# One chunk per turn from the start, and the gates and scans of block 7 moved up, in a recurrence-plus-maxout kernel

## Chip, cores, metric

The kernel runs on one core of a Trainium2 chip (trn2). The metric is the device time of one execution in microseconds (us). Kernels that are compared ran on the same chip in alternating rounds. A difference of 1 us is 0.26% here, so single executions mean little.

## The reference

```
sig = 1 / (1 + exp(-f_logit));  f = lb + (1 - lb) * sig;  i = 1 - f       # x, f_logit: (4, 6144, 256) fp32
for t in range(S):  h = f[:, t] * h + i[:, t] * x[:, t];  y[:, t] = h      # a recurrence per channel
h1 = y @ w1;  h2 = y @ w2                                                  # (24576, 256) @ (256, 1024)
out = maximum(h1, h2) @ w_out                                              # (1024, 256), fp32 out
```

## The kernel before

The 24576 tokens are 48 blocks of 512. Blocks 0 to 3 are chunks 0 to 3, loaded straight into SBUF. From block 4 on, two blocks are a *pair* and come as one chunk of 1024 tokens: pair 2 (blocks 4, 5) is chunk 4, pair 3 (blocks 6, 7) is chunk 5, and so on to chunk 25. A chunk takes these steps:

1. **Cast** (`fetch`): a DMA issued by POOL (GpSimd) reads fp32 and writes fp16 to one of two scratch areas in HBM, once for `f_logit` and once for `x`.
2. **Transpose** (`cross`): a DMA issued by SP (SyncE) turns each half into SBUF, with channels on the partitions (`fT`, `xT`). POOL waits for `fT`, then issues the next chunk's cast. That closes a loop: cast, transpose, next cast.
3. **Gate** on ACT (ScalarE): a sigmoid in four pieces, two for each block. Piece q covers time half q // 2 of the chunk and channel half q % 2.
4. On DVE (VectorE): **decay** and **drive** (small elementwise), then two **scans** for each block. `scan10` and `scan11` are the two channel halves of the pair's second block.
5. **First layer** on TensorE, 512 columns for each matmul, with a relu on ACT.
6. **Second layer**. From pair 2 on, the two blocks of a pair share seven products instead of eight. Their inputs are four **sums** of relu results, made on DVE (`sum3`, `sum1`, `sum2`, `sum4`, 1.4 us each). The sevenths of pair p run while the first layer of pair p + 1 runs.

TensorE instructions of a stage stand in 16 *slots*. `seq` holds (key, DVE work); slot n emits the work whose key is below 9(n + 1). Every engine takes its instructions in the order in which this loop emits them.

```
    def cross(*cs):
        if len(cs) > 1:                       # only cross(4, 5)
            nc.sync.dma_start(out=seen[:], in_=scratch[1][cs[-1] % NSCR][CH - 1 : CH, 0:16])
        for c in cs:
            for s in range(2):
                dst = inpool.tile([P, KC, CH], HALF, name=("fT", "xT")[s])
                nc.sync.dma_start_transpose(out=dst[:], in_=scratch[s][c % NSCR][:])
                held[c, s] = dst
        pool_waits(held[cs[-1], 0][:, 0, 0:1])
        if cs[-1] + 1 < NCHUNK:
            for s in range(2):
                fetch(cs[-1] + 1, s)
    # ... (cut)
        for p in range(PAIR0, NPAIR):         # PAIR0 = 2
            first = p == PAIR0
            more = p + 1 < NPAIR
            seq = [(27, scans[p]["scan10"]), (36, scans[p]["scan11"]), (112, lambda: sum3(p))]
            if more:
                scans[p + 1] = pair_scans(p + 1)
                seq += [(64, scans[p + 1]["decay0"]), (66, scans[p + 1]["drive0"]),
                        (70, scans[p + 1]["scan00"]), (84, scans[p + 1]["scan01"]),
                        (131, scans[p + 1]["decay1"]), (133, scans[p + 1]["drive1"])]
            if not first:
                seq += [(9, lambda: sum1(p - 1)), (18, lambda: sum2(p - 1)), (50, lambda: sum4(p - 1))]
                queue += sevenths(p - 1)
            seq.sort(key=lambda e: e[0])
            gates = {4: 0, 6: 1, 12: 2, 14: 3} if more else {}
            for slot in range(2 * FC):
                first_layer(2 * p + slot // FC, slot % FC)
                # ... (cut: evictions of block 3, the steps of the sevenths)
                if slot == 2 and p + 3 < NPAIR:
                    cross(blocks[2 * p + 6][3])
                if slot in gates:
                    pair_gate(p + 1, gates[slot])
                while seq and seq[0][0] < (slot + 1) * 9:
                    seq.pop(0)[1]()
```

Of the kernel before, what the change touches and what calls it, by code (L numbers as in the profile page):

```python
# [10 lines left out]
HALF = mybir.dt.float16  # L11
# [3 lines left out]
P = 128  # L15
# [3 lines left out]
def kernel(  # L19
# [10 lines left out]
    nc = tc.nc  # L30
# [4 lines left out]
    KC = D // P  # L35
    FC = DFF // P
    TB = 512
    CH = 1024
# [5 lines left out]
    blocks = []  # L44
    for b in range(B):
# [3 lines left out]
        for nt in sizes:  # L49
            first = len(blocks)  # L50
# [5 lines left out]
    NCHUNK = len(chunks)  # L56
# [4 lines left out]
    PAIR0 = 2  # L61
    NPAIR = NBLK // 2
    KH = FC // 2

    const = ctx.enter_context(tc.tile_pool(name="const", bufs=1))
# [4 lines left out]
    inpool = ctx.enter_context(tc.tile_pool(name="inp", bufs=4))  # L70
# [12 lines left out]
    NSCR = 2  # L83
# [8 lines left out]
    held = {}  # L92
# [3 lines left out]
    def fetch(c, s):  # L96
        b, t0, nt, _ = chunks[c]
        src = srcs[s][b, t0 : t0 + nt, :]
        if by_xbar(c, s):
            nc.gpsimd.dma_start(  # L100
                out=pieces(scratch[s][c % NSCR][:]), in_=pieces(src)
            )
        else:
            nat = inpool.tile([P, TB // P, D], HALF, name=("fT", "xT")[s])
            nc.gpsimd.dma_start(
                out=nat[:].rearrange("p i d -> p (i d)"),
                in_=src.rearrange("(p i) d -> p (i d)", p=P),
            )
            held[c, s] = nat
# [31 lines left out]
                    )  # L141
            raws[k, s] = dst[:].rearrange("p k i m -> p k m i")

    def cross(*cs):


        if len(cs) > 1:
            nc.sync.dma_start(
                out=seen[:], in_=scratch[1][cs[-1] % NSCR][CH - 1 : CH, 0:16]
            )  # L150
        for c in cs:
            for s in range(2):
                dst = inpool.tile([P, KC, CH], HALF, name=("fT", "xT")[s])
                nc.sync.dma_start_transpose(out=dst[:], in_=scratch[s][c % NSCR][:])
                held[c, s] = dst
        pool_waits(held[cs[-1], 0][:, 0, 0:1])
        if cs[-1] + 1 < NCHUNK:
            for s in range(2):
                fetch(cs[-1] + 1, s)

    def turn_steps(j):
        b, t0, nb, c, o = blocks[j]
# [156 lines left out]
    om = const.tile([P, KC], FP32)  # L319
    nom = const.tile([P, KC], FP32)  # L320
    lbc = const.tile([P, KC], FP32)
    seen = const.tile([1, 16], HALF)
    waited = const.tile([P, 1], FP32)
    warm = const.tile([P, 1], FP32)
    wob = wpool.tile([P, FC, D], HALF)
# [21 lines left out]
    def pool_waits(t):  # L347
        nc.gpsimd.tensor_copy(out=waited[:], in_=t)  # L348
# [315 lines left out]
    with tc.manual_schedule():  # L664
        nc.scalar.dma_start(out=lbc[:], in_=lower_bound.rearrange("(h p) -> p h", p=P))
        nc.vector.tensor_copy(out=ident[:], in_=ident_f[:])
        nc.scalar.activation(out=warm[:], in_=ident_f[:, 0:1], func=AF.Sigmoid)
        fetch_first(0)
        fetch_first(1)
        for g in range(NG):  # L670
            fetch_w(g)
        pool_waits(w1n[0][:, 0, 0:1])
        nc.gpsimd.dma_start(
            out=wob[:].rearrange("p (g q) c -> p g (q c)", g=NG),
            in_=moe_w_out.rearrange("(g p q) c -> p g (q c)", g=NG, q=NQ),
        )
        for c in range(1, 6):
            for s in range(2):
                fetch(c, s)
        wt = ps_d.tile([P, 2, 2 * TB], HALF, name="dT")  # L680
        for q in range(8):
            nc.tensor.transpose(wt[:, 0, 0:P], ident[:], ident[:])
        first_bf16(0, 0, nc.vector.tensor_copy)
        first_bf16(0, 1, nc.vector.tensor_copy)
        nc.vector.tensor_scalar_add(out=nom[:], in0=lbc[:], scalar1=-1.0)
        nc.vector.tensor_scalar(
            out=om[:], in0=lbc[:], scalar1=-1.0, scalar2=1.0, op0=ALU.mult, op1=ALU.add
        )
        first_turn(0)
        first_recurrence(0)  # L690
        first_bf16(1, 0, nc.scalar.copy)
        first_bf16(1, 1, nc.scalar.copy)
        first_turn(1)
        first_recurrence(1)
        for q in range(24):
            nc.tensor.transpose(wt[:, 0, 0:P], ident[:], ident[:])
        scale_w1(0)
        half_w1(0, nc.scalar.copy)
        scale_w1(1)
        pt0 = turn_w1(0)  # L700
        for pair in range(2):
            make_wd(0, pair)
            for fc in range(2 * pair, 2 * pair + 2):
                first_layer(0, fc)
        half_w1(1, nc.vector.tensor_copy)
        pt1 = turn_w1(1)
        for pair in range(2):
            make_wd(1, pair)
            for fc in range(4 + 2 * pair, 6 + 2 * pair):
                first_layer(0, fc)  # L710
        keep_w1T(0, pt0)
        keep_w1T(1, pt1)
        steps = turn_steps(1)
        make_w13(0)
        turn(steps[:8])
        gate(1)
        make_w13(1)
        turn(steps[8:])
        for step in scan_steps(1):
            step()  # L720
        cross(4, 5)
        for fc in range(FC):
            if fc == 4:
                turn(turn_steps(2))
                gate(2)
            if fc == 6:
                first_layer(1, 0)
                first_layer(1, 1)
            if fc < 7:
                second_layer(0, fc)  # L730
        for step in scan_steps(2):
            step()
        for step in make_sevens():
            step()
        for fc in range(2, FC):
            first_layer(1, fc)
            if fc == 3:
                second_layer(0, 7)
        turn(turn_steps(3))
        gate(3)  # L740
        early = scan_steps(3)
        for fc in range(FC):
            first_layer(2, fc)
            second_layer(1, fc)
            if fc < 4:
                early[fc]()
        cross(6)
        scans = {PAIR0: pair_scans(PAIR0)}
        gates = {0: 0, 1: 1, 4: 2, 5: 3}
        order = {  # L750
            2: ("decay0", "drive0"),
            3: ("scan00",),
            4: ("scan01",),
            6: ("decay1",),
            7: ("drive1",),
        }
        for fc in range(FC):
            first_layer(3, fc)
            second_layer(2, fc)
            if fc in gates:  # L760
                pair_gate(PAIR0, gates[fc])
            for t in order.get(fc, ()):
                scans[PAIR0][t]()

        queue, due = [], 0
        pieces3, piece = (1, 3, 5, 9, 11, 13, 15), 0
        for p in range(PAIR0, NPAIR):
            first = p == PAIR0
            more = p + 1 < NPAIR
            seq = [  # L770
                (27, scans[p]["scan10"]),
                (36, scans[p]["scan11"]),
                (112, lambda: sum3(p)),
            ]
            if more:
                scans[p + 1] = pair_scans(p + 1)
                seq += [
                    (64, scans[p + 1]["decay0"]),
                    (66, scans[p + 1]["drive0"]),
                    (70, scans[p + 1]["scan00"]),  # L780
                    (84, scans[p + 1]["scan01"]),
                    (131, scans[p + 1]["decay1"]),
                    (133, scans[p + 1]["drive1"]),
                ]
            if not first:
                seq += [
                    (9, lambda: sum1(p - 1)),
                    (18, lambda: sum2(p - 1)),
                    (50, lambda: sum4(p - 1)),
                ]  # L790
                queue += sevenths(p - 1)
            seq.sort(key=lambda e: e[0])
            gates = {4: 0, 6: 1, 12: 2, 14: 3} if more else {}
            for slot in range(2 * FC):
                first_layer(2 * p + slot // FC, slot % FC)
                if first and slot in pieces3 or p == PAIR0 + 1 and slot == 1:
                    second_layer(2 * PAIR0 - 1, piece)
                    piece += 1
                if p > PAIR0 + 1 or (p == PAIR0 + 1 and slot >= LAG):
                    due += NSEV / (2 * FC)  # L800
                    while due >= 1:
                        due -= 1
                        queue.pop(0)()
                if slot == 2 and p + 3 < NPAIR:
                    cross(blocks[2 * p + 6][3])
                if slot in gates:
                    pair_gate(p + 1, gates[slot])
                while seq and seq[0][0] < (slot + 1) * 9:
                    seq.pop(0)[1]()
        for step in queue:  # L810
            step()
        p = NPAIR - 1
        sum1(p)
        sum2(p)
        sum4(p)
        for step in sevenths(p):
            step()
# [30 lines left out]
```

## Time and profile before

| | before |
|---|---|
| time, median of 4 runs beside the changed kernel | 379.67 us (379.19 to 379.68) |
| span of the profiled execution | 377.7 us |
| all 4136 matmuls at their back-to-back spacing (estimate) | 363.1 us |
| TensorE starts later than that spacing, sum | 8.0 us |
| of that, between 20 and 360 us | 0.4 us |

From the profile's page (span; busy time and share; the chain that ended last, by engine):

```profile
span 377.7 us, 9593 instructions
PE 367.9 (97%) x4136; PEld 279.8 (74%) x4136; DVE 338.7 (90%) x410; ACT 302.4 (80%) x410; POOL 35.6 (9%) x79
...
PE 94%; DVE 3%; DMA 1%; issue 0%; SPq 0%; ACT 0%; DVEq 0%
```

TensorE is the limit, and busy time alone cannot tell how tight it is, so I used starts. In the timeline a run of matmuls that waits for nothing starts one every 0.216 us at 512 columns and every 0.056 us at 128. A *late start* below is the spacing of two starts minus that value. The one late start in the middle of the run is here.

61.99 - 61.37 - 0.216 = 0.40 us late: the first layer of block 7 waits for `scan11`. DVE, over the stretch before it (start, length, line, operation; in brackets its idle time and what ended it), has hardly a gap:

```profile
53.18 1.47 DVE L506 TENSOR_TENSOR S<-r 128x2560 f16<-128x2560 f16 x1
54.56 0.61 DVE L213 TENSOR_SCALAR ff<-u,nom 128x512 f16<-128x512 f16 x2
55.09 0.69 DVE L223 TENSOR_TENSOR v<-u,xT 128x1024 f16<-128x1024 f16 x1
56.08 0.69 DVE L496 COPY osb<-ps 128x512 f32<-128x512 f32 x1 [0.30 <-PE ps L487]
56.68 1.48 DVE L506 TENSOR_TENSOR S<-r 128x2560 f16<-128x2560 f16 x1
58.08 1.48 DVE L506 TENSOR_TENSOR S<-r,S 128x2560 f16<-128x2560 f16 x1
59.48 2.45 DVE L230 TENSOR_TENSOR_SCAN r<-ff,r,v 128x512 f16<-128x512 f16 x2
```

In order: `sum3`, decay, drive, the last eviction of block 3, `sum1` (56.68), `sum2` (58.08), `scan10` and `scan11` (59.48). `scan11` ends at 61.93, 0.35 us after it is wanted at 61.58.

The chain that ended last runs through just this piece (start, us, what):

```profile
56.08 0.69 DVE osb L496
56.77 2.80 DVE S L506 x2
59.57 2.38 DVE r L230 x2
61.95 0.04 issue
61.99 0.38 PE dT L441
```

SP's queue, first part (issue time, length of the issue): the tiny read `seen`, four transposes, then stores mixed with transposes.

```profile
32.59 0.30 SPq L148 DMA_DIRECT2D seen<-scr  x1
32.99 1.69 SPq L154 DMA_TRANSPOSE fT<-scr  x1
34.78 2.92 SPq L154 DMA_TRANSPOSE xT<-scr  x1
37.80 2.22 SPq L154 DMA_TRANSPOSE fT<-scr  x1
...
51.48 2.64 SPq L154 DMA_TRANSPOSE fT<-scr  x1
```

### The profile page before, as it was taken

To read this page: it belongs to the slowest core of one execution; us is meant where nothing else is said; L and a number is where in the kernel's file an instruction comes from. 1 tells how busy PE (TensorE), PEld (TensorE's weight loads), DVE (VectorE), ACT (ScalarE), POOL (GpSimd) and SP (SyncE) were. 2 spreads that over 40 slices of the span, in tenths; PEclk is the share of its full clock that TensorE was granted. 3 is DMA by queue.
4 is the path that set the end of the run, shared out by engine and by line. 5 is a ranking of instruction groups with operands and counts; after the bars stand their busy time and mean duration, and the time that the engine had idled before them with its cause. 6 is when DMAs were issued, how large, how long until landed. Compare 5 with 4: busy or idle time off the path is not lost.

```text
span 377.7 us, 9593 instructions
## 1 busy us (share of the span) xinstructions
PE 367.9 (97%) x4136; PEld 279.8 (74%) x4136; DVE 338.7 (90%) x410; ACT 302.4 (80%) x410; POOL 35.6 (9%) x79
## 2 busy tenths in 40 slices
PE   5999999999999999999999999999999999999994
PEld 3777767777777777777777777777777777777784
DVE  4796789999999999999999999999999999999772
ACT  5865897888888798888888887887988888889752
POOL 1500101110101101101201201011011001010000
PEclk9999999999999999999999999999999999999999
DMA  7996979998999999999999899999899899980223
GB/s 254 246 223 131 309 143 214 227 193 189 273 134 257 223 184 266 222 184 225 203 200 301 208 161 254 147 247 274 132 263 279 134 241 221 185 282 3 112 113 114
DMA packets 104813, 77.17 MB, mean 204 GB/s; under 512 B 93570, under 2 KB 95618, under 8 KB 104066
## 3 DMA queue, kind: packets, MB, share of 16 engines
q1 hardware_dynamic: 101538, 51.19, 60.5%
q0 software_dynamic: 2544, 25.17, 34.7%
q8 instruction: 32, 0.52, 0.6%
q10 hardware_dynamic: 688, 0.20, 0.2%
q14 instruction: 11, 0.09, 0.1%
HBM read 53.48 MB, written 48.23 MB: 269 GB/s over the span
## 4 chain that ended last, share of the span: by engine, by line
PE 94%; DVE 3%; DMA 1%; issue 0%; SPq 0%; ACT 0%; DVEq 0%
PE ps L650 44%; PE dT L441 43%; PE ps L487 5%; DMA osb<-in_x_dram 1%; DVE S L506 1%; PE ps L180 1%; DVE r L230 1%; DVE r L264 1%; PE ps L397 0%; DVE v L223 0%; DVE osb L568 0%; DVE osb L496 0%; PE ps L137 0%; DVE osb L589 0%; PE ps L383 0%
## 5 line engine op out<-in xcount | busy, mean ns | idle before, releaser
L449 ACT ACTIVATE r<-dT 128x1024 f16<-128x1024 f32 x192 | 195.9, 1023 | 53.4 <-PE dT L441 53.2
L441 PE MATMUL dT<-r,wd 128*128 128x512 f16 x768 | 225.5, 379 | 0.4 <-DVE r L230 0.2
L650 PEld LDWEIGHTS <-S 128*128 128x128 f16 x1760 | 115.5, 101 | 37.6 <-issue 0.5
L650 PEld LDWEIGHTS <-r 128*128 128x128 f16 x1320 | 90.9, 101 | 36.8 <-issue 0.2
L230 DVE TENSOR_TENSOR_SCAN r<-ff,r,v 128x512 f16<-128x512 f16 x88 | 108.2, 1269 | 0.8
L650 PE MATMUL ps<-t,S 128*128 128x128 f16 x1320 | 101.6, 219 | 0.0
L506 DVE TENSOR_TENSOR S<-r 128x2560 f16<-128x2560 f16 x44 | 65.3, 1485 | 14.5 <-ACT r L449 14.4
L441 PEld LDWEIGHTS <-wd 128*128 128x128 f16 x768 | 67.6, 113 | 5.2 <-DVE wd L365 1.2
L650 PE MATMUL ps<-wob,r 128*128 128x128 f16 x704 | 69.9, 219 | 0.0
L506 DVE TENSOR_TENSOR S<-r,S 128x2560 f16<-128x2560 f16 x44 | 64.8, 1473 | 0.0
L285 ACT ACTIVATE u<-fT 128x512 f16<-128x512 f16 x88 | 56.0, 637 | 1.3 <-DMA fT<-scr 1.3
L213 DVE TENSOR_SCALAR ff<-u,nom 128x512 f16<-128x512 f16 (+1 forms) x98 | 31.5, 344 | 8.5 <-ACT u L285 3.7
L650 PE MATMUL ps<-w,r 128*128 128x128 f16 x176 | 38.5, 219 | 0.0
L348 POOL CAST waited<-fT 128x1 f32<-128x1 f16 x21 | 8.8, 418 | 282.8 <-DMA fT<-scr 282.8
L650 PE MATMUL ps<-t,r 128*128 128x128 f16 x430 | 34.1, 219 | 0.1
L568 DVE TENSOR_TENSOR osb<-ps,sn 128x512 f32<-128x512 f32 x44 | 30.1, 683 | 3.2 <-PE ps L650 3.2
L650 PE MATMUL ps<-wob,S 128*128 128x128 f16 x352 | 32.6, 219 | 0.0
L223 DVE TENSOR_TENSOR v<-u,xT 128x1024 f16<-128x1024 f16 x44 | 30.0, 682 | 0.0
L556 ACT COPY sn<-ps 128x512 f32<-128x512 f32 x44 | 25.8, 587 | 2.4 <-PE ps L650 2.4
L566 ACT COPY osb<-ps 128x512 f32<-128x512 f32 x43 | 25.0, 582 | 0.8 <-PE ps L650 0.8
L487 PEld LDWEIGHTS <-r 128*128 128x128 f16 x160 | 16.0, 101 | 6.6
L650 PE MATMUL ps<-w,S 128*128 128x128 f16 x88 | 19.3, 219 | 0.0
(58 smaller groups left out, 131.9 us busy)
## 6 DMA issues: line engine op xcount, KB each, us to landing
out_dram<-osb SPq DMA_DIRECT2D x46, 512.0 KB, 3.8
scr<-in_f_logit_dram POOLq DMA_DIRECT2D x22, 512.0 KB, 7.9
scr<-in_x_dram POOLq DMA_DIRECT2D x22, 512.0 KB, 10.5
r<-in_moe_w_dram SPq DMA_DIRECT2D x4, 512.0 KB, 6.9
fT<-in_f_logit_dram POOLq DMA_DIRECT2D x3, 256.0 KB, 7.9
xT<-in_x_dram POOLq DMA_DIRECT2D x3, 256.0 KB, 8.5
out_dram<-osb SPq DMA_DIRECT2D x3, 256.0 KB, 2.6
osb<-in_f_logit_dram SPq DMA_DIRECT2D x2, 256.0 KB, 4.5
```

Source lines behind the costliest of these rows:

```text
L213: nc.vector.tensor_scalar(out=ff[:, h, cols], in0=u[:, h, cols], scalar1=nom[:, h : h + 1], scalar2=1.0, op0=ALU.mult, op1=ALU.add,)
L223: nc.vector.tensor_tensor(out=like(v[:, :, cols], xT), in0=like(u[:, :, cols], xT), in1=xT, op=ALU.mult,)
L230: nc.vector.tensor_tensor_scan(out=y_of(j, h), data0=ff[:, h, o : o + TB], data1=v[:, h, o : o + TB], initial=0.0 if t0 == 0 else y_of(j - ...
L285: nc.scalar.activation(out=mids[p + NBLK, "u"][:, h, cols], in_=held[c, 0][:, h, cols], func=AF.Sigmoid, scale=-1.0,)
L441: nc.tensor.matmul(dT[:, fc % 2, :], lhsT=wd[:, kc, unit_cols(fc)], rhs=y_of(j, kc), start=(kc == 0), stop=(kc == KC - 1),)
L449: nc.scalar.activation(out=rts[j, k][:, g - 1 : g + 1, :].rearrange("p q (i m) -> p q i m", m=P), in_=dT[:].rearrange("p q (m i) -> p q i ...
L487: nc.tensor.matmul(ps[:, r, :], lhsT=left, rhs=right, start=(s == 0 and r == 0), stop=(s == n - 1 and r == 1), skip_group_check=True,)
L506: nc.vector.tensor_tensor(out=t[:], in0=a, in1=b, op=op)
L556: nc.scalar.copy(out=t[:], in_=bank[b][:])
L566: nc.scalar.copy(out=dst, in_=bank[b][:])
L568: nc.vector.tensor_tensor(out=dst, in0=bank[b][:], in1=snap[name][:], op=ALU.add)
L650: nc.tensor.matmul(bank[b][:, i, :], lhsT=a[:, k, cols], rhs=w, start=fresh, stop=after is not None, skip_group_check=True,)
```

## The change

Its intent: handle every chunk alike, one for each turn. Chunk 4 is cast alone and transposed as soon as it has landed; chunk 5 follows. Each later transpose is issued one stage later in program order, so two more stores stand ahead of it in SP's queue. To close the hole at 61 us, gates 2 and 3, decay and drive of block 7 move up, `scan10` goes into the stage before, and `scan11` moves to slot 1.

```diff
-    def cross(*cs):
-        if len(cs) > 1:
-            nc.sync.dma_start(out=seen[:], ...)        # waits for chunk 5's cast
-        for c in cs: ...
+    def cross(c):                                      # one chunk
...
-        for c in range(1, 6):
+        for c in range(1, 5):                          # first casts
...
-        cross(4, 5)
+        cross(4)
...
-        cross(6)
+        cross(5)
...
-                (27, scans[p]["scan10"]),
-                (36, scans[p]["scan11"]),
+                (12 if p == PAIR0 + 1 else 36, scans[p]["scan11"]),
+            if p != PAIR0 + 1:
+                seq.append((27, scans[p]["scan10"]))
+            if first:
+                seq.append((126, scans[p + 1]["scan10"]))
...
-                    (131, scans[p + 1]["decay1"]),
-                    (133, scans[p + 1]["drive1"]),
+                    (110 if first else 131, scans[p + 1]["decay1"]),
+                    (111 if first else 133, scans[p + 1]["drive1"]),
...
-            gates = {4: 0, 6: 1, 12: 2, 14: 3} if more else {}
+            gates = {4: 0, 6: 1, 10 if first else 12: 2, 12 if first else 14: 3}
...
-                if slot == 2 and p + 3 < NPAIR:
-                    cross(blocks[2 * p + 6][3])
+                if slot == 2 and p + 2 < NPAIR:
+                    cross(blocks[2 * p + 4][3])
```

(Shortened; `if more` also moves to the place where a gate is emitted.)

More of the change, by code (lines that the diff above doesn't have):

```diff
@@ L142, in first_turn @@
             raws[k, s] = dst[:].rearrange("p k i m -> p k m i")
-    def cross(*cs):
-        if len(cs) > 1:
-            nc.sync.dma_start(
-                out=seen[:], in_=scratch[1][cs[-1] % NSCR][CH - 1 : CH, 0:16]
-            )
-        for c in cs:
-            for s in range(2):
-                dst = inpool.tile([P, KC, CH], HALF, name=("fT", "xT")[s])
-                nc.sync.dma_start_transpose(out=dst[:], in_=scratch[s][c % NSCR][:])
-                held[c, s] = dst
-        pool_waits(held[cs[-1], 0][:, 0, 0:1])
-        if cs[-1] + 1 < NCHUNK:
-            for s in range(2):
-                fetch(cs[-1] + 1, s)
+    def cross(c):
+        for s in range(2):
+            dst = inpool.tile([P, KC, CH], HALF, name=("fT", "xT")[s])
+            nc.sync.dma_start_transpose(out=dst[:], in_=scratch[s][c % NSCR][:])
+            held[c, s] = dst
+        pool_waits(held[c, 0][:, 0, 0:1])
+        if c + 1 < NCHUNK:
+            for s in range(2):
+                fetch(c + 1, s)
     def turn_steps(j):
@@ L321 @@
     lbc = const.tile([P, KC], FP32)
-    seen = const.tile([1, 16], HALF)
     waited = const.tile([P, 1], FP32)
@@ L769 @@
             more = p + 1 < NPAIR
+            if more:
+                scans[p + 1] = pair_scans(p + 1)
             seq = [
-                (27, scans[p]["scan10"]),
-                (36, scans[p]["scan11"]),
+                (12 if p == PAIR0 + 1 else 36, scans[p]["scan11"]),
                 (112, lambda: sum3(p)),
             ]
+            if p != PAIR0 + 1:
+                seq.append((27, scans[p]["scan10"]))
+            if first:
+                seq.append((126, scans[p + 1]["scan10"]))
             if more:
-                scans[p + 1] = pair_scans(p + 1)
                 seq += [
@@ L803 @@
                         queue.pop(0)()
-                if slot == 2 and p + 3 < NPAIR:
-                    cross(blocks[2 * p + 6][3])
-                if slot in gates:
+                if slot == 2 and p + 2 < NPAIR:
+                    cross(blocks[2 * p + 4][3])
+                if more and slot in gates:
                     pair_gate(p + 1, gates[slot])
```

## The prediction

> **What bounds it now.** TensorE: the page gives PE 97% busy, and the chain that ended last is 94% PE. The Trainium skill, "Perfetto Trace Analysis", Identifying the Most-Contended Engine, says that matmul busy time does not show closeness to roofline, so I read starts in the timeline: back to back, 512-column matmuls start every 0.216 us, those of 128 columns every 0.056, of 256 every 0.11. All 4136 at these spacings are an estimated 363 of the 377.7 us. Later starts add 8 us, nearly all before 12 us or in the last 12 us. Between them is one hole: at 61.4 us TensorE waits 0.4 us (0.24 us idle in the record) for block 7's scan, the end of a DVE chain in the chain of waits (two sums 2.8 us, two scans 2.4 us).
>
> Behind TensorE runs a DMA loop: cast a chunk, transpose its f half, POOL sees that, next cast. In the queue timeline the f transposes are 12.2 to 16.6 us apart, mean 14.4 from chunk 6 on; a pair stage on TensorE takes 14.73 us (ACT gates 88.87 to 103.60). The f transpose lands before its first gate by 0.1 us (chunk 4), 4.7 (5), 2.5 (6), 4.7 (7), then 4.4 to 8.4.
>
> **What the change does.** No arithmetic changes; the order on TensorE is the same. Gone is the tiny read that held the first transposes until chunk 5's cast landed (32.6 us).
> - Chunk 4: its casts land at 25.3/27.7 us, so f transposed lands near 31, not 37.8. ACT's wait of 1.3 us goes; TensorE did not wait: worth 0.
> - Chunk 5: cast from 31 instead of 16, f transposed near 43.5 to 44 (before 42.4); its gate is at 47.1.
> - Chunk 6: about 1 us later, near 57.5 against a gate at 59.0. The thinnest place.
> - Later, each transpose stands behind two more stores in SP's queue. They are ready about 2 slots into the stage (ACT copy at 86.3), transposes start near 90 when the cast lands: not binding.
> - Blocks 6 and 7: gates, decay and drive two slots earlier, one scan in the stage before, the other ahead of the sum: block 7 is scanned about 3 us earlier, so the hole of 0.4 us should close.
>
> The Trainium skill, "DMA: Bandwidth & Descriptors", Issuing engines are not separate DMA queues, says DMAs of all issuers run on the same 16 engines and interleave. The trace agrees: casts land 2.4 us apart in the first burst, but take 7 to 8 us from issue in the loop. Moved stores shift landings by a few us; the slack should take it.
>
> **Prediction.** 379.66 - 0.4 + 0.1 (chance of a short stall at chunk 6 or 7) = 379.3 us, 80% range 378.6 to 381.2. Faster by over 2%: 0.01; within 2%: 0.96; slower by over 2%: 0.03.
>
> **What would show it.** Right: TensorE's idle at 61 us gone, stages still 14.73 us, head and tail unchanged, f transposes of chunks 5 to 7 within 2 us of before, loop 14 to 15 us, no new wait for fT or xT. Wrong: ACT waiting over 1 us for fT or DVE for xT, then PE waiting; or loop periods over 14.73 us with slack falling steadily.
>
> **What would make it wrong.** The loop averages only 0.3 us under a stage: if serial work or moved stores lengthen it, the slack drains and late stages stall by some us. Or chunk 6 lands 3 us later than I reckon: 1 to 2 us slower. Or the earlier gates delay a relu in ACT's order and open a PE wait in pair 2's stage.

## More of the kernel before

TensorE timeline of before (start, length, line, operation; in brackets its idle time and what ended it):

```profile
58.23 0.22 PE L650 MATMUL ps<-w,r 128*128 128x128 f16 x1
58.29 0.50 PE L650 MATMUL ps<-t,S 128*128 128x128 f16 x6
...
59.99 0.61 PE L650 MATMUL ps<-t,S 128*128 128x128 f16 x8
...
61.37 0.38 PE L441 MATMUL dT<-r,wd 128*128 128x512 f16 x1
61.99 0.38 PE L441 MATMUL dT<-r,wd 128*128 128x512 f16 x1 [0.24 <-DVE r L230]
```

The line of 58.29 is the first product that reads `sum1` (`ps<-t,S`). `sum2` is first read in the line of 59.99, after five more matmuls of the `sum1` product, at about 60.27 us.

`sum1` ends at 58.16, 0.13 us before TensorE reads it. `sum2` ends at 59.56, 0.71 us before.

## The result, and the profile after

The changed kernel takes 380.73 us (median of 4 runs, 380.32 to 381.06) against 379.67 us. The ratio is 1.003, with a 95% interval of 1.0013 to 1.0048. Ratios here are the mean of one kernel's fast runs over the mean of the other's of the same rounds, so they are not quite the ratio of the medians. The time lies in the predicted range and within 2%, but the kernel became 1.1 us slower where I expected it 0.4 us faster. That it still fell into the range was luck: the upper part of the range stood for other losses (a drained slack, a late chunk 6, a delayed relu), and none of these cost time in the change.

The page after, and all that TensorE waited for after the first microseconds (who, whom, us in total, times, longest):

```profile
span 379.3 us, 9594 instructions
PE 368.5 (97%) x4136; PEld 280.3 (74%) x4136; DVE 339.0 (89%) x410; ACT 302.6 (80%) x410; POOL 39.5 (10%) x80
...
PE 92%; DVE 3%; DMA 1%; ACT 1%; issue 1%; SPq 0%; DVEq 0%; ACTq 0%
```

```profile
PE ps L644 <- DVE S L500: 1.0, 2, 0.6
```

The wait for the scan is gone. In its place are two waits for sums (`S`). TensorE timeline of after; L644 and L435 are the lines that were L650 and L441:

```profile
58.73 0.22 PE L644 MATMUL ps<-w,r 128*128 128x128 f16 x1
59.50 0.51 PE L644 MATMUL ps<-t,S 128*128 128x128 f16 x6 [0.56 <-DVE S L500]
...
61.21 0.44 PE L644 MATMUL ps<-t,S 128*128 128x128 f16 x5
62.08 0.34 PE L644 MATMUL ps<-t,S 128*128 128x128 f16 x3 [0.42 <-DVE S L500]
62.26 0.59 PE L435 MATMUL dT<-r,wd 128*128 128x512 f16 x2
```

The late starts are 59.50 - 58.73 - 0.056 = 0.72 us and 62.08 - 61.21 - 5 x 0.056 = 0.59 us, together 1.31 us where before had 0.40: a net loss of 0.9 us. DVE timeline of after:

```profile
54.18 0.69 DVE L218 TENSOR_TENSOR v<-u,xT 128x1024 f16<-128x1024 f16 x1
54.78 1.49 DVE L500 TENSOR_TENSOR S<-r 128x2560 f16<-128x2560 f16 x1
56.18 1.28 DVE L225 TENSOR_TENSOR_SCAN r<-ff,r,v 128x512 f16<-128x512 f16 x1
57.38 0.67 DVE L490 COPY osb<-ps 128x512 f32<-128x512 f32 x1
57.96 1.48 DVE L500 TENSOR_TENSOR S<-r 128x2560 f16<-128x2560 f16 x1
59.36 1.28 DVE L225 TENSOR_TENSOR_SCAN r<-ff,r,v 128x512 f16<-128x512 f16 x1
60.55 2.99 DVE L500 TENSOR_TENSOR S<-r,S 128x2560 f16<-128x2560 f16 x2
```

The same work, in another order: `scan10` (56.18) now stands ahead of `sum1` (57.96), and `scan11` (59.36) ahead of `sum2` (60.55). DVE has no gap left, so it even ends `sum2` about as early as it ended `scan11` before. But TensorE reads the sums before it reads the scans.

SP's queue after: chunk 4's transposes start 7 us earlier, and `seen` is gone.

```profile
25.54 2.38 SPq L149 DMA_TRANSPOSE fT<-scr  x1
28.02 2.02 SPq L149 DMA_TRANSPOSE xT<-scr  x1
30.13 7.55 SPq L454 DMA_DIRECT2D out_dram<-osb  x2
37.79 4.14 SPq L149 DMA_TRANSPOSE fT<-scr  x1
...
51.72 3.20 SPq L149 DMA_TRANSPOSE fT<-scr  x1
```

The profiled execution of after was the slowest of its four (381.06 us). Its late starts sum to 9.4 us against 8.0. Of these 1.4 us, 0.9 are the waits above. About 0.5 lie before 20 us, where the first inputs and weights arrive and where the change has not acted yet.

### The profile page after: what moved, and what is told of

Read it like the earlier page. It is cut to its first block, busy times and chain, and to the rows that moved or that the text cites. A ratio compares the mean times of both kernels' runs of the same rounds, so it can differ in the third digit from the quotient of the medians.

```text
span 379.3 us, 9594 instructions
## 1 busy us (share of the span) xinstructions
PE 368.5 (97%) x4136; PEld 280.3 (74%) x4136; DVE 339.0 (89%) x410; ACT 302.6 (80%) x410; POOL 39.5 (10%) x80
## 4 chain that ended last, share of the span: by engine, by line
PE 92%; DVE 3%; DMA 1%; ACT 1%; issue 1%; SPq 0%; DVEq 0%; ACTq 0%
PE ps L644 44%; PE dT L435 42%; PE ps L481 4%; DMA osb<-in_x_dram 1%; DVE S L500 1%; DVE r L225 1%; PE ps L175 1%; PE dT L690 1%; PE ps L391 0%; PE ps L377 0%; SPq L117 0%; DVE osb L490 0%; DVE v L218 0%; ACT u L280 0%; ACT r L443 0%
## 5 line engine op out<-in xcount | busy, mean ns | idle before, releaser
L435 PE MATMUL dT<-r,wd 128*128 128x512 f16 x768 | 225.8, 380 | 0.0
L644 PEld LDWEIGHTS <-S 128*128 128x128 f16 x1760 | 115.5, 101 | 38.5 <-DVE S L500 1.5
L644 PEld LDWEIGHTS <-r 128*128 128x128 f16 x1320 | 90.9, 101 | 36.8 <-issue 0.2
L644 PE MATMUL ps<-t,S 128*128 128x128 f16 x1320 | 101.8, 219 | 1.0 <-DVE S L500 1.0
L435 PEld LDWEIGHTS <-wd 128*128 128x128 f16 x768 | 67.8, 113 | 5.3 <-issue 0.5
L644 PE MATMUL ps<-wob,r 128*128 128x128 f16 x704 | 69.9, 219 | 0.0
L342 POOL CAST waited<-fT 128x1 f32<-128x1 f16 x22 | 13.7, 622 | 288.3 <-DMA fT<-scr 288.3
L644 PE MATMUL ps<-w,r 128*128 128x128 f16 x176 | 38.5, 219 | 0.0
L644 PE MATMUL ps<-t,r 128*128 128x128 f16 x430 | 34.1, 219 | 0.1
L562 DVE TENSOR_TENSOR osb<-ps,sn 128x512 f32<-128x512 f32 x44 | 30.1, 684 | 3.2 <-PE ps L644 3.2
L644 PE MATMUL ps<-wob,S 128*128 128x128 f16 x352 | 32.6, 219 | 0.0
L218 DVE TENSOR_TENSOR v<-u,xT 128x1024 f16<-128x1024 f16 x44 | 30.1, 685 | 0.0
L644 PE MATMUL ps<-w,S 128*128 128x128 f16 x88 | 19.3, 219 | 0.0
```

What stands on the lines that cost most here:

```text
L218: nc.vector.tensor_tensor(out=like(v[:, :, cols], xT), in0=like(u[:, :, cols], xT), in1=xT, op=ALU.mult,)
L435: nc.tensor.matmul(dT[:, fc % 2, :], lhsT=wd[:, kc, unit_cols(fc)], rhs=y_of(j, kc), start=(kc == 0), stop=(kc == KC - 1),)
L562: nc.vector.tensor_tensor(out=dst, in0=bank[b][:], in1=snap[name][:], op=ALU.add)
L644: nc.tensor.matmul(bank[b][:, i, :], lhsT=a[:, k, cols], rhs=w, start=fresh, stop=after is not None, skip_group_check=True,)
```

## Experiments

Two theories were set up:

- **Theory 1:** the order on DVE costs the time, because the two scans stand ahead of two sums that TensorE wants sooner.
- **Theory 2:** the chunk part costs it, through a later cast of chunk 5, a slower loop, or stores in other places.

Eleven kernels ran, and all gave correct outputs. "Late starts" are from each one's trace, between 20 and 360 us and over 0.1 us; the time given with one is the start of the matmul before it. The kernels of one chip call share their runs of before.

| kernel | median us | before, same rounds | ratio (95%) | late starts in the trace (us) |
|---|---|---|---|---|
| after_again | 380.65 | 379.79 | 1.0027 (1.0007 to 1.0046) | 0.72, 0.59 for sums |
| order_only | 380.40 | 379.79 | 1.0014 (1.0000 to 1.0027) | 0.72, 0.59 for sums; 0.13 at 43.6 |
| chunks_only | 379.58 | 379.79 | 0.9992 (0.9978 to 1.0006) | 0.40 for the scan; 0.16 at 297 |
| sum_in_the_gap | 379.41 | 379.79 | 0.9990 (0.9976 to 1.0004) | 0.27 at 39.5, 0.59 at 43.8, 0.41 at 49.2 |
| scans_both_first | 381.01 | 379.41 | 1.0038 (1.0026 to 1.0050) | 1.89 for `sum1`; 0.19 at 43.6 |
| sums_first | 379.46 | 379.41 | 1.0011 (0.9984 to 1.0037) | 0.41 for the scan |
| queue_order_back | 380.43 | 379.41 | 1.0023 (1.0011 to 1.0036) | 0.72, 0.59 for sums |
| early_chunk4_sum_in_gap | 379.31 | 379.41 | 0.9992 (0.9976 to 1.0008) | 1.65 at 171.5 |
| change_mended | 378.97 | 379.55 | 0.9987 (0.9973 to 1.0002) | 0.42 at 68.4 |
| six_out_buffers | 379.05 | 379.55 | 0.9987 (0.9975 to 1.0000) | none |
| early_chunk4_again | 379.17 | 379.55 | 0.9994 (0.9978 to 1.0010) | none |

### The change once more: after_again

No edit.

> The changed kernel itself, once more, on the same chip as the three below. Both theories: 0.8 to 1.2 us longer than before; in the trace TensorE starts late by about 0.7 us at the first product of the sum of pair 2 (near 58.7 us) and by 0.6 us at the second (near 61.4 us), and the wait of 0.4 us for block 7's scan is absent. The loop of f transposes has a mean period of 14.7 to 14.9 us. If the loss in the first 15 us (0.45 us more late starts in the first trace) is not there again, that part was run-to-run scatter.

Measured: 380.65 against 379.79 us, and the two late starts are again 0.72 and 0.59 us, at 58.0 and 60.7 us. The sum of late starts is 8.6 us this time, so the extra in the first 20 us did not come back: it was scatter between executions.

### Only the order: order_only

```diff
--- before
-                (27, scans[p]["scan10"]),
-                (36, scans[p]["scan11"]),
+                (12 if p == PAIR0 + 1 else 36, scans[p]["scan11"]),
+            if p != PAIR0 + 1: seq.append((27, scans[p]["scan10"]))
+            if first: seq.append((126, scans[p + 1]["scan10"]))
... and the changed keys of decay1 and drive1 and the changed gate slots; cross as before
```

> Only the moved gates and scans, the chunks as before. Theory 1 (the two scans now stand ahead of the two sums on DVE, and TensorE needs the sums sooner): it loses what the whole change loses, 0.7 to 1.1 us, with the two late starts of about 0.7 and 0.6 us in place of the 0.4 us one. Theory 2 (casting chunk 5 late and the new queue order cost the time): within 0.3 us of before, or faster by 0.4 us, because the scan hole closes.

Measured: 0.6 us slower by medians, a little less than expected. The interval begins at 1.0000, so the time alone hardly tells this kernel from before; the trace decides. It has exactly the changed kernel's pair of late starts. What TensorE waited for in order_only:

```profile
PE ps L650 <- DVE S L506: 1.0, 2, 0.6
```

### Only the chunks: chunks_only

```diff
--- after
+                (27, scans[p]["scan10"]),
+                (36, scans[p]["scan11"]),
-  (the moved scans, decay1, drive1 and gates, all back as before; cross as changed)
```

> Only one chunk per turn, the gates and scans as before. Theory 1: within 0.3 us of before, with the one late start of 0.4 us for block 7's scan near 61.5 us. Theory 2: 0.7 to 1.1 us slower. Either way the period of the f transposes should be near 14.8 us and the slack of the last chunks 1 to 3 us, as in the changed kernel, if it is the chunks part that slowed the loop.

Measured: 0.2 us below before by medians with an interval that includes 1, and the old late start of 0.40 us for the scan. What TensorE waited for in chunks_only, after the first microseconds:

```profile
PE dT L435 <- DVE r L225: 0.2, 1, 0.2
```

So the loss sits in the order part, as theory 1 says, and theory 2 falls as the cause of the time. The loop, though, did slow down here too (see queue_order_back).

### The dose doubled: scans_both_first

```diff
--- order_only
-                (12 if p == PAIR0 + 1 else 36, scans[p]["scan11"]),
+                (3 if p == PAIR0 + 1 else 36, scans[p]["scan11"]),
```

> The dose doubled: chunks as before, and both scans of block 7's pair half stand ahead of both sums on DVE (in the change one scan stands ahead of each sum). Theory 1: the first sum ends 1.2 us later than in the order-only kernel, so TensorE's late start at the first sum's product near 58.2 us grows from 0.72 to about 1.9 us, the second one near 60.9 us goes to 0 to 0.2 us; 1.3 to 1.7 us slower than before. If the position ahead of the sums were not the cause, it stays at about 0.7 us slower.

Measured: 381.01 against 379.41 us, 1.6 us slower. One late start of 1.89 us at the first sum, none at the second. What TensorE waited for in scans_both_first:

```profile
PE ps L650 <- DVE S L506: 1.7, 1, 1.7
```

The size follows from the margins read before. Two scans take 2.4 us; `sum1` had 0.13 us to spare and DVE regains its 0.30 us gap, so 2.4 - 0.13 - 0.30 = 1.97 us is the estimate and 1.89 is measured. With one scan ahead: 1.2 - 0.13 - 0.30 = 0.77, measured 0.72. For `sum2` in the change: 2.4 - 0.71 - 0.30 - 0.72 (TensorE is already that much later) = 0.67, measured 0.59.

### The change with the scans behind the sums: sums_first

```diff
--- after
-                (12 if p == PAIR0 + 1 else 36, scans[p]["scan11"]),
+                (27, scans[p]["scan10"]),
+                (36, scans[p]["scan11"]),
-            if p != PAIR0 + 1:
-                seq.append((27, scans[p]["scan10"]))
-            if first:
-                seq.append((126, scans[p + 1]["scan10"]))
```

> The changed kernel with its chunks and its earlier gates, decay and drive, but both scans put back behind both sums. Theory 1: the loss goes, within 0.3 us of before, one late start of 0.3 to 0.45 us for the scan near 61 us, none for the sums. Rival (the earlier gates or drive cost the time, not the scans): 0.7 to 1.1 us slower, as the change.

Measured: median 379.46 against 379.41 us. One of its six runs took 382.74 us, which widens the interval and makes the ratio itself inconclusive; its profile was taken in another run. The trace has one late start, 0.41 us, for the scan again, and none for sums. So in the trace the earlier gates, decay and drive cost nothing; only the place of the scans does.

### The transposes ahead of the stores again: queue_order_back

```diff
--- after
         cross(4)
+        cross(5)
...
-        cross(5)
+        cross(6)
...
-                if slot == 2 and p + 2 < NPAIR:
-                    cross(blocks[2 * p + 4][3])
+                if slot == 2 and p + 3 < NPAIR:
+                    cross(blocks[2 * p + 6][3])
```

> The changed kernel with each transpose put back one stage earlier in SP's queue, so that the two newest stores follow it as before; chunk 4 is still cast alone and gates and scans stay as changed. Time as the change, 0.7 to 1.1 us slower than before, since the loop is not on TensorE's path. If the stores ahead of the transposes slowed the loop, its period comes back to 14.2 to 14.5 us and the slack of the last chunks to 6 to 11 us; if the serial start of chunks 4 and 5 did, it stays at 14.8 us and the slack at 1 to 3 us.

Measured: 1.0 us slower than before, as the change. The loop came back to its old speed. Below, the loop's period is the mean distance of the landings of the f transposes from chunk 6 to chunk 25, and slack is the time from that landing to the chunk's first gate:

| kernel | stores stand | period, us | slack of chunk 6 | of chunk 7 | of chunk 25 |
|---|---|---|---|---|---|
| before | behind | 14.47 | 2.5 | 4.7 | 8.0 |
| order_only | behind | 14.39 | 2.0 | 5.2 | 10.0 |
| queue_order_back | behind | 14.41 | 1.8 | 5.6 | 9.1 |
| after | ahead | 14.79 | 2.6 | 4.9 | 2.6 |
| after_again | ahead | 14.77 | 1.2 | 4.6 | 1.8 |
| chunks_only | ahead | 14.91 | 2.5 | 3.6 | 0.0 |
| sums_first | ahead | 14.76 | 2.8 | 4.2 | 2.7 |

A stage on TensorE takes 14.73 us. With the stores ahead of the transposes the loop takes slightly longer than that. The stage between the gates of chunks 6 and 7 holds the late starts studied here, so the slack is best followed from chunk 7. With the stores behind, it grows; with the stores ahead, it shrinks by 1.5 to 3.6 us over 18 chunks, though not evenly (in sums_first it is 0.8 us at chunk 14). In chunks_only it is used up from chunk 22 on: ACT waited up to 0.8 us for `fT` there and TensorE started 0.16 us late at 297 us. queue_order_back keeps chunk 4 alone and still has the short period, so the serial start is not the cause; the place of the stores is. The stores do not act by holding a transpose back in SP's queue: from chunk 7 on, the f transpose is issued on average 0.05 us after its cast has landed in before and 0.07 us in after. By which contention among the DMAs they act, no run here shows.

### A first attempt to do better: sum_in_the_gap

```diff
--- before
-                    (9, lambda: sum1(p - 1)),
+                    (8 if p == PAIR0 + 1 else 9, lambda: sum1(p - 1)),
-            gates = {4: 0, 6: 1, 12: 2, 14: 3} if more else {}
+            gates = {4: (0, 1), 12: (2,), 14: (3,)} if first else {4: (0,), 6: (1,), 12: (2,), 14: (3,)}
... (cut: the loop that now takes these lists of gates)
```

> The kernel before with two moves in pair 2's and pair 3's stage: gate 1 right after gate 0, so that DVE does not wait about 0.9 us for it near 48.5 us, and the first sum ahead of the last eviction of block 3, in a DVE idle of 0.3 us at 55.8 us; both scans stay behind the sums. Theory 1 (DVE is the engine that limits 49 to 62 us, and what counts is which result TensorE needs first): no late start over 0.1 us between 50 and 65 us, 0.3 to 0.4 us faster than before. If the order were not the cause, no gain.

Measured: half a miss. The hole at 61 us closed, but the trace has three others, and the interval includes 1. The 0.41 us at 49.2 us comes with my moved gate: two gates now run ahead of a relu, which starts 1.04 us after the first gate (47.74 to 48.78); in before it starts 0.52 us after it (47.13 to 47.65). The 0.27 and 0.59 us near 40 to 44 us come with chunk 4: its f half landed at 38.16 us in this run and ACT waited 1.91 us for it (1.33 in before). Traces with the old start have a late start near 43.6 us of 0 (before), 0.13, 0.19 and 0.59 us; none of the nine with chunk 4 alone has one. So the chunk part seems to remove something that shows only in some executions; no run isolates it.

### Both lessons together: early_chunk4_sum_in_gap, early_chunk4_again, six_out_buffers, change_mended

The first two are one kernel: queue_order_back with gates and scans as before and `sum1` moved by `(8 if p == PAIR0 + 1 else 9, ...)` ahead of the last eviction, into DVE's gap of 0.3 us.

> A candidate better than both: chunk 4 cast alone (no ACT wait for it), transposes ahead of the stores as before, gates and scans as before, and only the first sum of pair 2 moved ahead of the last eviction of block 3, into DVE's idle of 0.3 us. Theory 1: the late start for the scan near 61 us falls from 0.4 to about 0.1 us, nothing else opens; 0.2 to 0.5 us faster than before, which the interval may not resolve; no stall near 40 to 44 us.

> The early-chunk-4 candidate with four output buffers again, on the chip of the two above. Its six runs were from 378.8 to 380.7 us; if late stores stop it in some executions, it is spread like that again, wider than the one with six buffers.

Measured: 379.31 and 379.17 us, 0.1 and 0.4 us below before by medians; both intervals include 1. In the DVE timeline of early_chunk4_sum_in_gap, `sum1` now stands ahead of the eviction, with no gap between them:

```profile
55.50 1.49 DVE L500 TENSOR_TENSOR S<-r 128x2560 f16<-128x2560 f16 x1
56.91 0.68 DVE L490 COPY osb<-ps 128x512 f32<-128x512 f32 x1
```

No late start between 20 and 70 us in either trace, so the hole is closed. But the first one's profiled run (380.68 us) has a stop of 1.65 us at 171.5 us. DVE timeline of early_chunk4_sum_in_gap there:

```profile
168.74 1.49 DVE L500 TENSOR_TENSOR S<-r 128x2560 f16<-128x2560 f16 x1 [0.55 <-ACT r L443]
172.46 0.69 DVE L562 TENSOR_TENSOR osb<-ps,sn 128x512 f32<-128x512 f32 x1 [2.23 <-DMA out_dram<-osb]
```

An eviction waited for a store to leave its output buffer; that store was issued at 160.1 and landed at 172.4 us. It had not been held up in SP's queue: the eviction that it stores ended at 160.01 us, so the 12.3 us passed between issue and landing. A store as slow (12.2 us, issued at 302 us) is in the trace of before too, where no eviction waited for it. So that the old queue order causes such stops is not shown. One of the second six runs was long as well (380.96 us), without a profile of it, so these runs are spread as widely as the first six.

```diff
--- early_chunk4_sum_in_gap
-    opool = ctx.enter_context(tc.tile_pool(name="opool", bufs=4))
+    opool = ctx.enter_context(tc.tile_pool(name="opool", bufs=6))
```

> The early-chunk-4 candidate with six output buffers instead of four, nothing else. If its stop of 1.65 us near 171 us came from a store standing behind a transpose in SP's queue while all four output buffers were taken, no eviction waits for a store in this one, the longest run comes down from 380.7 to below 379.8 us, and the mean is 0.3 to 0.7 us faster than before. If the stop had another cause, runs near 380.5 us remain.

Measured: 379.05 against 379.55 us, no late start in the trace and no wait for a store. But one of five runs took 380.02 us, so my bound of 379.8 failed. Before has such runs too (380.36 in these rounds), so whether late stores make the long runs stays open.

The last one is the change with its mistake taken out: chunks_only with `sum1` moved by that same key 8.

> The change's chunk part (chunk 4 alone, one chunk per turn, stores ahead of the transposes) with the gates and scans of before and the first sum of pair 2 ahead of the last eviction. Theory 1: the late start near 61 us is under 0.15 us and no sum is waited for; 0.2 to 0.5 us faster than before. The loop's period is 14.7 to 14.9 us and its slack falls to 0 to 3 us, so late gates may cost up to 0.2 us in some executions; no eviction waits for a store.

Measured: 378.97 against 379.55 us, the lowest median of all, about 0.6 us below before. The upper end of the interval is 1.0002, so that it beats before is likely and not proven. No late start at 61 us and no wait for a sum; one of 0.42 us at 68.4 us, where chunk 6's x half landed late (63.6 us) and DVE waited 0.37 us for it. Chunk 6 is the thinnest place, as predicted.

## Why the prediction was right or wrong

- **What bounds the kernel: right.** TensorE's 363 us of back-to-back work is the same in all traces, and the differences could be found as late starts: the spans of all thirteen traces, each less its late starts, agree within 0.2 us (369.6 to 369.8). With only 8 us of late starts in before, nearly all of them in the head and the tail, this change could not gain 2%. The Trainium skill, "TensorE: Matmul & The Clock Gate", Step-by-step: what each phase is for, says that matmuls stay in program order. The trace agrees: while the products waited 0.72 us for `sum1`, the first-layer matmuls behind them, whose inputs were ready, waited too.
- **The step that failed:** "block 7 is scanned about 3 us earlier, so the hole of 0.4 us should close", the -0.4 in the sum. The hole did close, and the first scan starts 3.3 us earlier (59.48 to 56.18); the second, for which TensorE had waited, ends only 1.3 us earlier (61.93 to 60.64), since `sum1` stands between them. I had even written that a scan goes "ahead of the sum", and did not ask when TensorE reads that sum. Its margin of 0.13 us stood in the trace of before. Two late starts of 0.72 and 0.59 us came instead: the term is +0.9 us, not -0.4. order_only, scans_both_first and sums_first show it by having the scans ahead, twice ahead, and back.
- **Chunk 4, "worth 0": right for the trace that I read, too small in general.** f landed at 30.1 us (predicted near 31), and ACT's wait went. But with the old start, three other traces lost 0.13 to 0.86 us around 40 to 44 us.
- **Chunks 5 and 6: nearly right.** Chunk 5's f half landed at 44.9 us (predicted 43.5 to 44), 2.5 us after before and so outside my 2 us. Chunk 6's landed at 56.9 (predicted 57.5). Neither was waited for.
- **Moved stores, "not binding": right for the time, wrong for the loop.** I named a loop above 14.73 us with steadily falling slack as a sign that I was wrong. The loop went to 14.8 us and the slack of the last chunks fell to 1 to 3 us. In the change it lasted to the end of the program, in chunks_only it did not. From 4.9 us at chunk 7 to 2.6 at chunk 25 it shrinks by 0.13 us for each chunk, so it would last some 20 chunks more (an estimate from these two slacks).
- **The shared DMA engines.** The packets in the trace of before bear out what the prediction cites of DMAs of several issuers: from 99 to 106 us SP's queue moved 1.42 MB and POOL's 0.75 MB side by side. How much they delay one another was not worked out.
- **"The earlier gates delay a relu and open a PE wait": did not happen** in the change (sums_first has nothing but the scan's late start), but my own gate move in sum_in_the_gap did just that.

## What to carry to other kernels

When an engine runs without gaps, moving one instruction up delays all that it passes: list, for each one passed, when it ends and when the limiting engine first reads it, and move nothing across a margin smaller than its own length. Here 1.2 us went across margins of 0.13 and 0.71 us to heal a lateness of 0.35 us; filling the engine's one gap of 0.3 us with the earliest-wanted piece healed it without a loser. And a loop with slack needs its period compared with the stage's, not only its slack at one place.

## What the Trainium skill lacked or had wrong

- "TensorE: Matmul & The Clock Gate", Back-to-back issue gap, gives a sustained spacing of about 81 ns at N = 128 and about 131 ns at N = 512 for streams of weight loads and matmuls, and calls N/2.4 + 2.5 ns the gap of isolated ones. Here a long stream of such pairs runs at 56 ns at 128 columns and 216 ns at 512 (nine matmuls in 0.50 us, two in 0.43 us in the chain of waits), which is the formula, not the sustained figures. The page does not agree with itself: its Step-by-step section gives 215.7 and 55.6 ns as measured, and that is what is seen here.
- "Perfetto Trace Analysis", Identifying the Most-Contended Engine, offers MFU (the share of the peak matmul rate that the kernel reaches) and weight-load busy time for TensorE. Weight-load busy time does not show a hole of 0.4 us: it is 279.8 us before and 280.3 us after. MFU was not worked out. The late starts against the back-to-back spacing showed it (8.0 against 9.4 us in all). The idle gaps of the record show the holes too, but too short: 0.24 us where the start was 0.40 us late, 0.56 for 0.72, 0.42 for 0.59.
- "DMA: Bandwidth & Descriptors", Issuing engines are not separate DMA queues, says that DMAs interleave on the same 16 engines. No page says how much the place of stores among transposes in one issuer's queue matters: here it moved a cast-and-transpose loop from 14.4 to 14.8 us, and single stores of 512 KB take far longer than others from issue to landing: 12.2 us for one in before, where the median is 3.8.
- No page has a rule for reordering on an engine without gaps; here one scan ahead cost 0.72 us and two cost 1.89.
